# Two decode attention blocks on one core: first loads ahead of the block, x on SP's queue, the store's wait behind the closing barrier

## The chip, the cores and the metric

The kernel runs on one core of one Trainium2 chip. The core has five engines that take their instructions independently of each other: TensorE (PE), VectorE (DVE), ScalarE (ACT), GpSimd (POOL) and SyncE (SP). Here SP does nothing but issue DMAs and wait. Data are moved by 16 DMA engines. The metric is the device time of one execution in microseconds; lower is better. A profiled execution shows the span from the program's first instruction to its last; the device time holds that and what lies around it.

## What is computed

Two attention blocks, A and B, each for one new token against a cache of 8192 positions and 32 heads of 128, in bf16. Their outputs, 512 numbers each, stand side by side in the result.

```python
B, Sq, D = x.shape                     # 1, 1, 512
H, Dh = 32, 128
q = (x @ wq).reshape(B, Sq, H, Dh).transpose(0, 2, 1, 3)
scores = jnp.einsum("bhqd,bhkd->bhqk", q, k_cache) * (Dh ** -0.5)
p = softmax(scores, axis=-1)
o = jnp.einsum("bhqk,bhkd->bhqd", p, v_cache)
return o.transpose(0, 2, 1, 3).reshape(B, Sq, H * Dh) @ wo
# result: concatenate([block(A), block(B)], axis=-1)
```

B is written for grouped heads, but has as many key heads as query heads, so both blocks have one shape. Each reads 64 MB of k, 64 MB of v (in units of 2^20 bytes), 4 MB of wq and 4 MB of wo: 285 million bytes in all.

## The kernel before

**Tiling.** The 64 heads are worked through in 16 groups of four heads (n = 0 to 15, eight for A, then eight for B). A group's k, and its v, is 8 MB: four heads by 32 partitions, and 256 positions by 128 numbers on each partition. k has two buffers (`kn`, taken in turn), v has one (`vn`). The weights have no room of their own: wq of A and of B lie in `vn` until the first v comes, wo lies in a buffer of `kn` at the end, and the two rows of x (`xrow`, 1 KB each) lie on partition 0 of buffer 1 of `kn`, where the k of group 1 goes later.

**Work of a group.** DVE multiplies k by q in four chunks, in place (`plan_mul`, line 337). PE adds the products up over eight slices with an identity matrix (`plan_red`, line 346), DVE finishes the sum (line 357). Then come the maximum, the exponential on ACT (line 394), and on PE the product with v (`plan_pv`, line 415). The product with v of group n - 1 runs within the work of group n.

**The first work.** x comes in two loads that ACT issues. PE spreads each row over all partitions with a row of ones (line 297), ACT copies the result to `xb` (line 301); the second copy is the mark `x_ready`. `plan_q` multiplies `xb` by wq (line 315), 16 matmuls for four groups, and ACT copies q to `qbc` (line 323). For A this is done ahead of the first group, for B within it.

**Order of the work.** Everything is written out by hand. A small planner (`_Plan`) holds a list of instructions and waits for each engine; `op` adds an instruction, `wait` a wait on a semaphore. `dma` adds a load or a store to an engine's list, at line 244 in the profile. At the end of the kernel each list is emitted within one `Block`, to which every engine branches at its start and at whose end all five meet at a barrier (line 174 in the profile). The program has a barrier of its own ahead of the kernel's first line (line 626).

**SP's list.** wq of A, k of group 0, wq of B; then k of group 1, which waits for `x_ready`, since x lies where it goes; then in turn v of group n, which waits until the buffer is read (v of group 0 waits until q of B is made), and k of group n + 2, which waits for the reduction of group n; then wo of both blocks in pieces, the last v in two pieces, and the store. The store of the 1024 results waits for the last copy on DVE (line 488), and SP waits for the store.

```python
def load_k(n):
    k_in[n] = dma("SP", flat(kn[:, n % NK]), quad(ks, n), s_k[n % NK],
                  [x_ready if n == KX else red_done.get((n - NK, NCH - 1))])

def load_wq(a):
    wq_in[a] = dma("SP", wq_buf[a], wqs[a].rearrange("(p c) n -> p (c n)", p=P), s_w[a])
```

Of the kernel before, what the change touches and what calls it, by code (L numbers as in the profile page):

```python
# [23 lines left out]
class _Plan:  # L24
# [6 lines left out]
    def wait(self, eng, mark):  # L31
        if mark is None:
            return
        ctr, val = mark
        if val <= 0 or self.waited.get((eng, ctr.name), 0) >= val:
            return
        self.waited[(eng, ctr.name)] = val
        self.prog[eng].append((None, ctr, val))

    def op(self, eng, fn, ctr=None, needs=(), inc=1):  # L40

        for m in needs:
            self.wait(eng, m)
        self.prog[eng].append((fn, ctr, inc))
        if ctr is None:
            return None
        ctr.n += inc
        return ctr, ctr.n


def _emit(e, items, slot=None):
    for fn, ctr, k in items:
        if fn is None:
            e.wait_ge(ctr.sem, k)
        elif isinstance(fn, tuple):
            which, fns = fn
            if slot is None:
                fns[which](e).then_inc(ctr.sem, k)
            else:
                with e.If_eq(slot, 0):  # L60
                    fns[0](e).then_inc(ctr.sem, k)
                with e.Else():
                    fns[1](e).then_inc(ctr.sem, k)
        elif ctr is None:
            fn(e)
        else:
            fn(e).then_inc(ctr.sem, k)


def _steps(items):  # L70


    out, waits = [], []
    for it in items:
        if it[0] is None:
            waits.append(it[1:])
        else:
            out.append((waits, it))
            waits = []
    assert not waits  # L80
    return out
# [48 lines left out]
def bass_concat_heads__mha_block_cached__gqa_block_cached__decode_kernel(  # L130
# [13 lines left out]
    xs = [A_x, B_x]  # L144
# [4 lines left out]
    NA = 2  # L149
# [13 lines left out]
    NK = 2  # L163
# [8 lines left out]
    VLAST = (0, T - CT, T)  # L172

    with ExitStack() as st:
        ec = st.enter_context
        block = ec(nc.Block())

        def sb(name, shape, dt):
            return ec(nc.sbuf_tensor(name, shape, dt))
# [4 lines left out]
        def flat(ap):  # L184
            return ap.rearrange("p t d -> p (t d)")
# [8 lines left out]
        xrow = flat(kn[0:1, KX])[:, 0:NA * D].rearrange("p (a d) -> p a d", a=NA)  # L194
# [19 lines left out]
        NQ = NOUT // P  # L214
        yT = sb("yT", [P, NA, NQ], BF16)
        out_q = sb("out_q", [NA * NQ, P], BF16)
# [11 lines left out]
        pl = _Plan()  # L228
        op, wait = pl.op, pl.wait

        def ctr(name):
            return _Ctr(nc, st, name)

        s_x = ctr("s_x")
# [3 lines left out]
        s_v = [ctr("s_v%d" % i) for i in range(len(VLAST) - 1)]  # L238
        s_out = ctr("s_out")
# [3 lines left out]
        def dma(eng, dst, src, c, needs=()):  # L243
            return op(eng, lambda e: e.dma_start(dst, src), c, needs, inc=16)  # L244


        def const(fn, needs=()):
# [5 lines left out]
            out=ident[:], in_=ones_bf[:], pattern=[[1, P]], compare_op=ALU.is_equal,  # L253
            fill=0.0, base=0, channel_multiplier=-1), [i_onesb])
        i_identf = const(lambda e: e.affine_select(
            out=ident_f[:], in_=ones_f[:], pattern=[[1, P]], compare_op=ALU.is_equal,
# [5 lines left out]
        i_pool = const(lambda e: e.memset(pt[:], 0.0))  # L262


        x_in = [dma("ACT", xrow[0:1, a, :], xs[a][0], s_x) for a in range(NA)][-1]
        k_in, v_in, wq_in, wo_in = {}, {}, {}, {}
        red_done, pv_done, q_done, wo_done = {}, {}, {}, {}

# [4 lines left out]
# [3 lines that stand above are left out]
# [7 lines left out]
        def load_wq(a):  # L283
            wq_in[a] = dma("SP", wq_buf[a], wqs[a].rearrange("(p c) n -> p (c n)", p=P), s_w[a])

        def load_wo(a, g):
# [2 lines left out]
            wo_in[a, g] = dma("SP", wo_sb[a][:, h0:h0 + n, :].rearrange("p j n -> p (j n)"), src,  # L289
                              s_wo[a][g], [red_done[NM - 2, NCH - 1]])  # L290


        for a in range(NA):
            def xmm(e, a=a):
# [5 lines left out]
            m = op("PE", xmm, c_pe, [x_in, i_onesb])  # L300
# [29 lines left out]
        turn = [None]  # L330
# [101 lines left out]
        def plan_sel():  # L432
            for g in RG:
                v = ident[:].rearrange("p (s j) -> p s j", j=g)
                op("DVE", lambda e, g=g, v=v: e.tensor_reduce(mask[g][:], v, AX.X, ALU.max),
                   c_dve, [i_ident])
                sel_ready[g] = op("DVE", lambda e, g=g, v=v: e.tensor_reduce(
                    jsel[g][:], v.rearrange("p s j -> p j s"), AX.X, ALU.max), c_dve)
# [45 lines left out]
        def plan_out():  # L484
            m = op("PE", lambda e: e.matmul(bmp[0:NA * NQ, 0:P], yT[:].rearrange("p a q -> p (a q)"),
                                            ident[:], start=True, stop=True),
                   c_pe, [qy_free[0], nb_done[NM - 1]])
            m = op("DVE", lambda e: e.tensor_copy(out_q[:], bmp[0:NA * NQ, 0:P]), c_dve, [m])
            done = dma("SP", out[0].rearrange("o (q n) -> (o q) n", q=NA * NQ), out_q[:], s_out, [m])
            wait("SP", done)  # L490


        L0, L1 = 1, NM
        cuts = {n: [] for n in range(L0, L1 + 1)}
        dcuts = []

        load_wq(0)
        load_k(0)
        load_wq(1)
        plan_sel()  # L500
        for j in range(QA // 4):
            plan_q(0, j)
# [56 lines left out]
        for g in range(BEFORE + 1, NB):  # L559
            plan_wo(1, g)  # L560
        plan_y(1)
        plan_out()

        for name, at in (("SP", block.sync), ("PE", block.tensor), ("ACT", block.scalar),
                         ("DVE", block.vector), ("POOL", block.gpsimd)):
            @at
            def _(e, name=name):
                prog = pl.prog[name]
                if name == "DVE":
                    ends = dcuts[::NK]  # L570
                    _emit(e, prog[:ends[0]])
                    lp = _Loop(e, [prog[x:y] for x, y in zip(ends, ends[1:])])
                    with e.Fori(0, len(ends) - 1) as turn[0]:
                        for k in range(len(lp.body)):
                            lp.emit(k, None)
                    turn[0] = None
                    _emit(e, prog[ends[-1]:])
                    return
                if name != "PE":
                    _emit(e, prog)  # L580
                    return
                _emit(e, prog[:cuts[L0][0]])
                lp = _Loop(e, [prog[cuts[n][0]:cuts[n + 1][0]] for n in range(L0, L1)])
                a, b = [len(_steps(prog[cuts[L0][0]:x])) for x in cuts[L0][1:]]
                final = _steps(prog[cuts[L1][1]:cuts[L1][2]])
                assert len(final) == b - a == len(VLAST)
                for k, (ws, it) in zip(range(a, b), final):
                    assert it[1:] == lp.body[k][1][1:]
                    have = lp.last[k] + ([(s_v[k - a - 1], 16)] if k > a + 1 else [])
                    assert all(w in have for w in ws)  # L590
                slot, left = e.alloc_register("slot"), e.alloc_register("left")
                e.reg_mov(slot, L0 % NK)
                e.reg_mov(left, L1 - L0)
                with e.Fori(0, 2) as again:
                    with e.Fori(0, (L1 - L0) - (L1 - L0 - 1) * again):
                        with e.If_ne(left, 0):
                            for k in range(a):
                                lp.emit(k, slot)
                        for k in range(a, b):
                            if k > a + 1:  # L600
                                with e.If_eq(left, 0):
                                    e.wait_ge(s_v[k - a - 1].sem, 16)
                            lp.emit(k, slot)
                        with e.If_ne(left, 0):
                            for k in range(b, len(lp.body)):
                                lp.emit(k, slot)
                            e.reg_sub(slot, 1, slot)
                        e.reg_sub(left, left, 1)
                    with e.If_eq(left, -1):
                        _emit(e, prog[cuts[L1][2]:])  # L610
                    with e.Else():
                        _emit(e, prog[cuts[L1][0]:cuts[L1][1]])


# [26 lines left out]
```

## Time and profile before

| | us |
|---|---|
| median of 3 runs | 667.87 (667.80 to 667.88) |
| span of the profiled execution | 666.3 |
| PE, DVE, ACT busy in it | 440.7, 340.2, 62.4 |
| first issue of a load on SP | 0.80 |
| issue of the store | 664.67 |

The profiled execution shows 666.3 us from the first to the last instruction. Its own device time is not recorded apart from the span; the median of the runs shown lies 1.57 us above that span, and what lies in between is not in the trace. The DMA engines are busy at nine tenths or more in 39 of the 40 slices of the span.

Rows of the timeline and of the chain begin with the start in us from the span's start and the duration in us; "SPq" is an instruction of SP's sequencer, and an issue of a DMA has the time that the issuing takes, not the transfer. "To landing" is the time from the issue until the last byte is reported. A row of waits has the us in total, how often, and the longest.

### The profile page before, as it was taken

The numbers are of one execution on the slowest core, as the hardware profiler recorded it, in microseconds if no ns is written. First come the engines' busy times: TensorE is split into PE (matmuls) and PEld (weight loads), VectorE is DVE, ScalarE is ACT, GpSimd is POOL, SyncE is SP. The second block draws the span as 40 slices with busy tenths as digits, with TensorE's granted clock in tenths as the row PEclk, the third lists the DMA queues.
The fourth block names the chain that finished last, engine by engine and source line by source line (L and its number), as shares of the span: only waits on it lengthen the run. The fifth ranks groups of instructions, "written<-read, shape, count | busy, mean of one in ns | idle before, by whom it ended". The sixth has DMA issues, their size and how long they took to land.

```text
span 666.3 us, 12449 instructions
## 1 busy us (share of the span) xinstructions
PE 440.7 (66%) x5646; PEld 252.4 (38%) x5646; DVE 340.2 (51%) x215; ACT 62.4 (9%) x151; POOL 2.8 (0%) x15
## 2 busy tenths in 40 slices
PE   2065875938487594848658484865948486685866
PEld 1022352615244261614425161442626144252645
DVE  1095818356381835638083563809256481925610
ACT  1002002020201002020200202020020202002020
POOL 1000000000000000000000000000000000000000
PEclk9678777769787775978777587877658797765875
DMA  9999999999999999999999999999999999999996
GB/s 378 437 445 438 438 431 433 409 437 441 441 429 433 441 441 425 417 437 441 441 421 441 441 433 429 417 441 441 441 421 441 437 433 429 421 441 441 407 454 274
DMA packets 6076, 285.33 MB, mean 428 GB/s; under 512 B 690, under 2 KB 948, under 8 KB 1204
## 3 DMA queue, kind: packets, MB, share of 16 engines
q1 hardware_dynamic: 6064, 285.22, 99.2%
q8 instruction: 6, 0.10, 0.1%
q14 instruction: 2, 0.02, 0.0%
q10 hardware_dynamic: 4, 0.00, 0.0%
HBM read 285.21 MB, written 0.00 MB: 428 GB/s over the span
## 4 chain that ended last, share of the span: by engine, by line
DMA 62%; PE 25%; DVE 10%; issue 2%; SPq 0%; DVEq 0%; another core or an unknown queue 0%; ACT 0%
DMA kn<-in_B_k_cache_dram 21%; DMA kn<-in_A_k_cache_dram 19%; PE rps L346 15%; DMA vn<-in_A_v_cache_dram 14%; PE acc L415 10%; DVE kn L337 9%; DMA vn<-in_B_v_cache_dram 5%; DMA kn<-in_B_wo_dram 4%; SPq L244 0%; DVE s_sb L357 0%; PE qyp L315 0%; DVEq L117 0%; PE misc L399 0%; ACT qbc L323 0%
## 5 line engine op out<-in xcount | busy, mean ns | idle before, releaser
L346 PE MATMUL rps<-kn,ident 128*128 128x512 bf16 x1024 | 294.5, 456 | 171.7 <-DVE kn L337 171.7
L337 DVE TENSOR_TENSOR kn<-kn,qbc 128x8192 bf16<-128x8192 bf16 x64 | 281.5, 4419 | 98.5 <-DMA kn<-in_A_k_cache_dram 59.0
L346 PEld LDWEIGHTS rps<-kn,ident 128*128 128x128 bf16 x1024 | 112.5, 114 | 340.6 <-issue 266.3
L415 PE MATMUL acc<-pt,vn 128*128 128x4 bf16 x4096 | 108.8, 165 | 5.6 <-DMA vn<-in_B_v_cache_dram 2.4
L415 PEld LDWEIGHTS acc<-pt,vn 128*128 128x128 bf16 x4096 | 108.3, 100 | 6.2 <-DMA vn<-in_B_v_cache_dram 2.7
L357 DVE TENSOR_REDUCE s_sb<-rps 128x64 f32<-128x512 f32 x64 | 44.0, 688 | 110.9 <-PE rps L346 110.9
L394 ACT ACTIVATE pt<-s_sb,negb 32x256 bf16<-32x256 f32 x64 | 54.8, 857 | 2.1 <-ACT negb L386 0.2
L386 ACT ACTIVATE negb<-bmp 128x1 f32<-128x1 f32 x16 | 2.7, 171 | 528.8 <-PE bmp L382 528.8
L424 DVE TENSOR_TENSOR oD<-acc,rinv 128x4 f32 (+1 forms) x16 | 2.6, 163 | 90.9 <-PE acc L415 90.9
L382 PE MATMUL bmp<-gm,hrow 1*128 1x1 f32 x128 | 17.0, 249 | 6.0 <-DVE gm L372 6.0
L382 PEld LDWEIGHTS bmp<-gm,hrow 1*128 1x128 f32 x128 | 15.6, 188 | 10.7 <-DVE gm L372 10.0
L369 PE MATMUL mtp<-ident_f,m 128*1 128x128 f32 x32 | 6.1, 271 | 19.8 <-DVE m L363 19.8
L394 ACT ACTIVATION_READ_ACCUMULATOR pt<-s_sb,negb 32x1 f32 x64 | 15.9, 248 | 0.0
L369 PEld LDWEIGHTS mtp<-ident_f,m 128*1 128x1 f32 x32 | 1.4, 81 | 27.7 <-DVE m L363 27.7
L473 PE MATMUL qyp<-o,kn 128*128 128x1 bf16 x248 | 7.4, 165 | 4.9 <-issue 3.5
L315 PE MATMUL qyp<-vn,xb 128*32 128x512 bf16 x64 | 5.9, 496 | 5.8 <-DMA vn<-in_A_wq_dram 4.3
L473 PEld LDWEIGHTS qyp<-o,kn 128*128 128x128 bf16 x248 | 7.0, 102 | 5.4 <-issue 3.9
L372 DVE TENSOR_REDUCE gm<-mtp 1x4 f32<-1x128 f32 x16 | 4.5, 279 | 7.6 <-PE mtp L369 7.6
L399 PEld LDWEIGHTS misc<-rsum,ones_f 128*128 128x128 f32 x32 | 6.2, 197 | 3.5 <-issue 1.4
L363 DVE TENSOR_REDUCE m<-s_sb 128x1 f32<-128x256 f32 x16 | 6.7, 420 | 0.5
L323 ACT CAST qbc<-qyp 128x512 bf16<-128x512 f32 x4 | 2.3, 586 | 43.0 <-PE qyp L315 43.0
L297 PE MATMUL misc<-ones_bf,kn 1*128 1x128 bf16 x4 | 0.6, 302 | 8.0 <-DMA kn<-in_B_x_dram 8.0
(36 smaller groups left out, 25.1 us busy)
## 6 DMA issues: line engine op xcount, KB each, us to landing
vn<-in_B_v_cache_dram SPq DMA_DIRECT2D x1, 6144.0 KB, 22.2
vn<-in_A_wq_dram SPq DMA_DIRECT2D x1, 4096.0 KB, 12.4
vn<-in_B_wq_dram SPq DMA_DIRECT2D x1, 4096.0 KB, 40.6
kn<-in_A_wo_dram SPq DMA_DIRECT2D x1, 4096.0 KB, 35.1
kn<-in_B_wo_dram SPq DMA_DIRECT2D x1, 2048.0 KB, 39.6
vn<-in_B_v_cache_dram SPq DMA_DIRECT2D x1, 2048.0 KB, 26.7
kn<-in_B_wo_dram SPq DMA_DIRECT2D x1, 1024.0 KB, 28.7
kn<-in_B_wo_dram SPq DMA_DIRECT2D x1, 512.0 KB, 29.5
```

The costliest lines, as they stand in the source:

```text
L315: r = e.matmul(qyp[hh * HP:(hh + 1) * HP, :].rearrange("p (i d) -> p i d", d=Dh), xb[:, a, c, hh * HP:(hh + 1) * HP], w, start=(c == 0), s ...
L337: mul_done[n, c] = op("DVE", lambda e: e.tensor_tensor(k, k, qbc[:, nth(n), :].broadcast_to([P, CT, Dh]), ALU.mult), c_mul, [k_in[n], qbc_ ...
L346: r = e.matmul(rps[:, c % 2, :].rearrange("p (t d) -> p t d", d=DW), ident[:], kn[:, i0, c * CT:(c + 1) * CT, i * DW:(i + 1) * DW], start= ...
L357: sr_done[n, c] = op("DVE", lambda e: e.tensor_reduce(s_sb[:, c * CT:(c + 1) * CT], rps[:, c % 2, :].rearrange("p (t d) -> p t d", d=DW), ...
L363: m_done[n] = op("DVE", lambda e: e.tensor_reduce(m1[:], s_sb[:], AX.X, ALU.max), c_dve, [sr_done[n, NCH - 1]])
L369: m = op("PE", lambda e: e.matmul(mtp[0:1, 0:P], m1[:], ident_f[:], start=True, stop=True), c_pe, [m_done[n], i_identf, gm_done.get(n - 1)])
L372: gm_done[n] = op("DVE", lambda e: e.tensor_reduce(gm[:], mtp[0:1, 0:P].rearrange("o (h p) -> o h p", h=G), AX.X, ALU.max), c_dve, [m, nb_ ...
L382: r = e.matmul(bmp[:, 0:1], hrow[0:1, h, :], gm[0:1, h:h + 1], start=(h == 0), stop=(h == G - 1))
L394: p_done[n] = op("ACT", lambda e, h=h, q=q: e.activation(pt[q, :, h], s_sb[q, :], AF.Exp, bias=negb[q, n:n + 1], scale=scale, accum_out=rs ...
L399: m = op("PE", lambda e: e.matmul(misc[:, 0:G], ones_f[:], rsum[:], start=True, stop=True), c_pe, [p_done[n], misc_free[0]])
L415: r = e.matmul(acc[:, 0:G], vn[:, t, :], pt[:, t, :], start=(t == 0), stop=(t == T - 1))
L473: r = e.matmul(qyp[:, i:i + 1], wo_sb[a][:, j, i * P:(i + 1) * P], (o2 if n > 1 else oD)[:, a, j:j + 1], start=(j == 0 and i == 0), stop=( ...
```

## The change

The block is opened later. The list of SP is cut: what stands in it when wq of A, the two rows of x, k of group 0 and wq of B are planned is emitted ahead of the block, and the rest within it. The lists of the other engines are emitted within the block as before. The rows of x move from ACT's list to SP's, behind wq of A. The wait for the store moves from SP's list to the line behind the block, so SP goes to the closing barrier when it has issued the store. The body of the block is indented by one step more; its lines are the same otherwise, and the lines of the kernel shift by one to four.

```diff
     with ExitStack() as st:
         ec = st.enter_context
-        block = ec(nc.Block())
...
-        x_in = [dma("ACT", xrow[0:1, a, :], xs[a][0], s_x) for a in range(NA)][-1]
         k_in, v_in, wq_in, wo_in = {}, {}, {}, {}
...
+        load_wq(0)
+        x_in = [dma("SP", xrow[0:1, a, :], xs[a][0], s_x) for a in range(NA)][-1]
 
         for a in range(NA):
             def xmm(e, a=a):
...
-            done = dma("SP", out[0].rearrange("o (q n) -> (o q) n", q=NA * NQ), out_q[:], s_out, [m])
-            wait("SP", done)
+            dma("SP", out[0].rearrange("o (q n) -> (o q) n", q=NA * NQ), out_q[:], s_out, [m])
...
-        load_wq(0)
         load_k(0)
         load_wq(1)
+        ahead = len(pl.prog["SP"])
         plan_sel()
...
-        for name, at in (("SP", block.sync), ("PE", block.tensor), ("ACT", block.scalar),
-                         ("DVE", block.vector), ("POOL", block.gpsimd)):
-            @at
-            def _(e, name=name):
-                prog = pl.prog[name]
+        _emit(nc.sync, pl.prog["SP"][:ahead])
+
+        with nc.Block() as block:
+            for name, at in (("SP", block.sync), ("PE", block.tensor), ("ACT", block.scalar),
+                             ("DVE", block.vector), ("POOL", block.gpsimd)):
+                @at
+                def _(e, name=name):
+                    prog = pl.prog[name][ahead if name == "SP" else 0:]
...
+        nc.sync.wait_ge(s_out.sem, s_out.n)
```

More of the change, by code (lines that the diff above doesn't have):

```diff
@@ L562, in bass_concat_heads__mha_block_cached__gqa_block_cached__decode_kernel @@
         plan_out()
-        for name, at in (("SP", block.sync), ("PE", block.tensor), ("ACT", block.scalar),
-                         ("DVE", block.vector), ("POOL", block.gpsimd)):
-            @at
-            def _(e, name=name):
-                prog = pl.prog[name]
[L569 to L597, printed above, removed]
-                                lp.emit(k, slot)
[L599 to L612, printed above, removed]
@@ new lines, in bass_concat_heads__mha_block_cached__gqa_block_cached__decode_kernel @@
+        _emit(nc.sync, pl.prog["SP"][:ahead])
[5 more added lines that the diff above has]
+                    prog = pl.prog[name][ahead if name == "SP" else 0:]
+                    if name == "DVE":
+                        ends = dcuts[::NK]
+                        _emit(e, prog[:ends[0]])
+                        lp = _Loop(e, [prog[x:y] for x, y in zip(ends, ends[1:])])
+                        with e.Fori(0, len(ends) - 1) as turn[0]:
+                            for k in range(len(lp.body)):
+                                lp.emit(k, None)
+                        turn[0] = None
+                        _emit(e, prog[ends[-1]:])
+                        return
+                    if name != "PE":
+                        _emit(e, prog)
+                        return
+                    _emit(e, prog[:cuts[L0][0]])
+                    lp = _Loop(e, [prog[cuts[n][0]:cuts[n + 1][0]] for n in range(L0, L1)])
+                    a, b = [len(_steps(prog[cuts[L0][0]:x])) for x in cuts[L0][1:]]
+                    final = _steps(prog[cuts[L1][1]:cuts[L1][2]])
+                    assert len(final) == b - a == len(VLAST)
+                    for k, (ws, it) in zip(range(a, b), final):
+                        assert it[1:] == lp.body[k][1][1:]
+                        have = lp.last[k] + ([(s_v[k - a - 1], 16)] if k > a + 1 else [])
+                        assert all(w in have for w in ws)
+                    slot, left = e.alloc_register("slot"), e.alloc_register("left")
+                    e.reg_mov(slot, L0 % NK)
+                    e.reg_mov(left, L1 - L0)
+                    with e.Fori(0, 2) as again:
+                        with e.Fori(0, (L1 - L0) - (L1 - L0 - 1) * again):
+                            with e.If_ne(left, 0):
+                                for k in range(a):
+                                    lp.emit(k, slot)
+                            for k in range(a, b):
+                                if k > a + 1:
+                                    with e.If_eq(left, 0):
+                                        e.wait_ge(s_v[k - a - 1].sem, 16)
+                                lp.emit(k, slot)
+                            with e.If_ne(left, 0):
+                                for k in range(b, len(lp.body)):
+                                    lp.emit(k, slot)
+                                e.reg_sub(slot, 1, slot)
+                            e.reg_sub(left, left, 1)
+                        with e.If_eq(left, -1):
+                            _emit(e, prog[cuts[L1][2]:])
+                        with e.Else():
+                            _emit(e, prog[cuts[L1][0]:cuts[L1][1]])
```

## The prediction

> **What bounds the kernel now.** I read the page from its chain of waits to the DMA rows, then the stretches by stage, and last the first 50 us and the last 3 us as timelines, since the change touches nothing in between.
>
> ```profile
> span 666.3 us, 12449 instructions
> DMA  9999999999999999999999999999999999999996
> q1 hardware_dynamic: 6064, 285.22, 99.2%
> q8 instruction: 6, 0.10, 0.1%
> q10 hardware_dynamic: 4, 0.00, 0.0%
> DMA 62%; PE 25%; DVE 10%; issue 2%; SPq 0%; DVEq 0%; another core or an unknown queue 0%; ACT 0%
> vn<-in_A_wq_dram SPq DMA_DIRECT2D x1, 4096.0 KB, 12.4
> vn<-in_B_wq_dram SPq DMA_DIRECT2D x1, 4096.0 KB, 40.6
> kn<-in_B_wo_dram SPq DMA_DIRECT2D x1, 1024.0 KB, 28.7
> ```
>
> ```profile
> core 0: us, PE busy (x) PEld busy (x) DVE busy (x) ACT busy (x) POOL busy (x), PEclk, DMA share, GB/s
> 0.00:2.00 2.00, 0.00 (x0) 0.00 (x0) 0.51 (x3) 0.41 (x1) 1.38 (x9) 1.00 0.64 164
> 62.50:604.50 542.00, 373.06 (x4648) 211.75 (x4648) 293.55 (x168) 51.93 (x131) 0.00 (x0) 0.76 1.00 433
> 653.58:666.30 12.72, 9.65 (x322) 9.08 (x322) 1.06 (x5) 0.00 (x0) 0.00 (x0) 0.50 0.63 258
> ```
>
> The kernel is a stream: 285 MB pass through one queue, SP's (q1), whose packets fill 99.2% of 16 engines' span. In the 542 us between the landing of the second k group and that of the last one the DMA share is 1.00 at 433 GB/s, while PE is busy for 373 us of 542 and DVE for 294. So nothing that PE, DVE or ACT wait for in between is worth time as long as the queue holds work. The time is made of three parts: what passes before the first packet, the stream, and what passes after the last landing. The change can gain in the first and the third alone, and lose only by leaving a hole in the stream or lengthening an end.
>
> **The first loads and the start.** SP's part of the chain of waits, and the timeline of the start:
>
> ```profile
> 0.74 0.07 issue
> 0.80 0.40 SPq L244
> 631.70 0.04 issue
> 634.11 29.37 DMA kn<-in_B_wo_dram
> ```
>
> ```profile
> start us, us, engine line op out<-in xcount [idle before <-releaser]
> 0.80 0.52 ACTq L244 DMA_DIRECT2D kn<-in_A_x_dram  x1
> 0.80 0.40 SPq L244 DMA_DIRECT2D vn<-in_A_wq_dram  x1
> 1.26 0.41 SPq L244 DMA_DIRECT2D kn<-in_A_k_cache_dram  x1
> 1.35 0.21 ACTq L244 DMA_DIRECT2D kn<-in_B_x_dram  x1
> 1.73 0.42 SPq L244 DMA_DIRECT2D vn<-in_B_wq_dram  x1
> 8.01 0.61 PE L297 MATMUL misc<-ones_bf,kn 1*128 1x128 bf16 x4 [8.01 <-DMA kn<-in_B_x_dram]
> 9.14 0.59 ACT L301 CAST xb<-qyp 128x512 bf16<-128x512 f32 x1
> 9.75 0.33 SPq L244 DMA_DIRECT2D kn<-in_A_k_cache_dram  x1
> 13.36 1.93 PE L315 MATMUL qyp<-vn,xb 128*32 128x512 bf16 x16 [4.31 <-DMA vn<-in_A_wq_dram]
> 17.90 0.58 ACT L323 CAST qbc<-qyp 128x512 bf16<-128x512 f32 x1 [1.96 <-PE qyp L315]
> 32.60 8.76 DVE L337 TENSOR_TENSOR kn<-kn,qbc 128x8192 bf16<-128x8192 bf16 x2 [28.82 <-DMA kn<-in_A_k_cache_dram]
> ...
> 632.22 2.33 SPq L244 DMA_DIRECT2D kn<-in_B_wo_dram  x5
> ```
>
> SP comes out of the start-up barrier of the program (line 626) and sets off wq of A at 0.80. Only the 0.07 us of "issue" ahead of it holds the branch into the block; the barrier, which comes ahead of the block in both kernels, stays. Between two instructions that SP issues back to back stand 0.04 us (the row at 631.70). So the branch that wq no longer waits for is worth 0.07 - 0.04 = **0.03 us**. Its bounds are 0, if what stands there is the barrier's own release, and 0.07.
>
> **x behind wq.** Now x goes out on ACT's queue (q10, 4 packets) at 0.80 and 1.35, beside wq, and the later one lands at about 8.0. On SP's queue it stands behind wq, which lands at 0.80 + 12.4 = 13.2. I put x at 13.3, 5.3 us later. From x to the end of the second cast is now 8.01 to 9.14 + 0.59 = 9.73, so 1.7 us: x_ready moves from 9.73 to 15.0. Two things wait for it.
> - q of A: today its matmuls start with wq at 13.36, and the last cast of the pair ends at 17.90 + 0.58 = 18.48, 5.1 us later. From 15.0 it ends at 20.1. The first multiply (line 337) needs k, which lands at 32.60. The cover is 12.5 us and the delay 1.6, so the cost is nothing; beyond the cover every microsecond would count in full, since k of group 2 may only go where the first group has been read.
> - k of group 1, whose wait on x_ready is the same in both kernels: SP issues it at 9.75 now and at 15.1 then. In the queue it stands behind k of group 0 and wq of B, whose data end at 1.73 + 40.6 = 42.3. The engines reach it 27 us after its new issue, so no hole opens. On SP nothing is queued behind that wait but v of group 0, which needs q of B and so wq of B anyway.
>
> PE's first matmuls (line 297) wait 5.3 us longer, and what stands behind them on PE needs wq, or k, which come no earlier. ACT loses two issues and waits for the same matmuls.
>
> **What else SP issues.** The two x instructions took 0.52 and 0.21 us on ACT; with two gaps of 0.04 they hold up k of group 0 and wq of B by 0.8 us, to about 2.0 and 2.5. The engines are busy with wq until 13.2, eleven microseconds beyond that, which covers it. In the queue itself two short transfers are new. What a transfer costs there beyond its bytes can be bounded at the end of the stream: the 1024 KB piece of wo, first of the five issues whose last one starts at 634.11, is issued at 632.22 and lands 28.7 us later, at 660.92; the last piece lands at 634.11 + 29.37 = 663.48. Between them 1024 KB land, in four transfers and 2.56 us; at 433 GB/s the bytes alone take 2.42. That is 0.035 us a transfer, so 0.07 for the pair, less what the same two packets take off the engines today from the other queue. I take **0**, with 0 and +0.15 (the pair at twice that) as bounds.
>
> **The end.** The closing rows: SP's waits, the instructions of the block's exit (line 174), and the timeline.
>
> ```profile
> SPq L174 <- DMA out_dram<-out_q: 0.9, 1, 0.9
> SPq L174 <- PEq L174: 0.2, 1, 0.2
> ```
>
> ```profile
> L174 SPq COMPARE_BRANCH  x1: 33/33/33, 665.9 to 665.9; - x1
> L174 SPq DRAIN  x1: 7/7/7, 666.1 to 666.1; - x1
> L174 SPq EVENT_SEMAPHORE  x1: 17/17/17, 666.2 to 666.2; - x1
> L174 PEldq EVENT_SEMAPHORE  x1: 51/51/51, 666.2 to 666.2; - x1
> ```
>
> ```profile
> 664.36 0.28 DVE L488 CAST out_q<-bmp 8x128 bf16<-8x128 f32 x1 [0.36 <-PE bmp L485]
> 664.67 0.37 SPq L244 DMA_DIRECT2D out_dram<-out_q  x1
> ```
>
> SP issues the store from 664.67 to 665.04 and waits 0.9 us, until 665.9. Only then do its branch out of the block, its drain and the barrier of five engines follow: from 665.9 to the span's end at 666.3, **0.37 us** with the row's rounding. In the new order these 0.37 us begin at 665.04 and are over by 665.45, under the flight of the store, which lands at 665.9 as before. What remains behind the landing is one wait instruction, 0.017 to 0.051 us by the rows of the same kind. The gain is 0.37 - 0.04 = **0.33 us**. Bounds: 0, if the program's end is set by something that follows SP's last instruction at a fixed distance from the barrier, and 0.9 + 0.37 = 1.27, if it is set by what follows on the other four engines, which are free at 665.45.
>
> **The sum.** 0.03 + 0 + 0.33 = 0.36 us less: the span goes from 666.3 to 665.9. The median of the runs, 667.87, is 1.57 us above the profiled span; no view of this trace shows what lies there, so I leave it as it is, and the time becomes 667.87 - 0.36 = **667.5 us**, 0.05% less. What a measurement of this kernel can tell from no change is about 0.2%, 1.34 us: the forecast is "the same".
>
> The Trainium skill (Runtime: NRT & Kernel Launch, section "The ~15µs preamble/postamble breakdown") has a barrier behind each kernel at which all engines are waited for. By that rule the four engines that are free early gain nothing by it, as SP still comes last, and the sum stays at 667.5; without it the sum could be as low as 667.87 - 1.27 - 0.03. No run here shows that barrier.
>
> **Rivals.**
> 1. *What follows on the other engines sets the end.* PE, ACT, DVE and POOL leave the closing barrier 0.9 us earlier than the span's gain alone would have it. If their own work behind the kernel is the longest, up to 1.27 + 0.03 us go: 666.6 us. For it speaks that 1.57 us lie outside the span; against it, that SP still has to come to its end after 665.9. That is 1.30 us, just inside 0.2%.
> 2. *Nothing is saved.* The start is set by the barrier and the end by the store's landing and a fixed tail behind it: 667.9 us. For it: the store takes as long as before (0.37 + 0.9), and it is the last thing in both orders. Against it: the exit at line 174 visibly starts behind the landing now.
> 3. *Slower: an instruction fetch falls on the DMA engine that ends last.* The place: the 16 engines are 99.2% busy with the one queue, so the one with the most foreign work ends last and releases the last piece of wo at 663.48. The 6 fetches of q8 take 0.1% of 16 engines' span, 0.001 x 666.3 x 16 = 10.7 us, so 1.8 us each (0.9 to 2.7 with the rounding of 0.1%). The change moves code between ACT's and SP's programs and places instructions ahead of the block. If that leads one fetch more to that engine, the end moves by 1.8 us, less the 0.36: 669.3. It decides from the point at which the fetched engine is behind all others; on any other engine it is covered. Against it: PE's and DVE's programs, the long ones, keep their instructions and order.
> 4. *Slower: x comes too late.* If x on SP's queue took not 13.3 but more than 13.3 + 12.5 = 25.8 us, the first multiply would wait. With x 2 us beyond that point: 667.5 + 2 = 669.5. Only a queue that ends x behind k of group 0 could do that; the queue's loads land in the order of their issue (wq of A at 13.2, k at 32.6, wq of B at 42.3).
>
> The Trainium skill (Runtime: NRT & Kernel Launch, section "Instruction fetch mechanics") has instructions streamed in 16 KiB blocks by each engine's own DMA queue, and a taken branch beyond the loaded pages pay for a fetch. That is the rule behind rival 3 which speaks against moving code; q8's 0.10 MB in 6 packets agree with its block size, and the branch into the block, 0.07 us, shows no such stall.
>
> **How the numbers follow.** Forecast 0.66, own range 667.2 to 667.75 (0.07 and 0.6 us gained to the bound of the short transfers). Rival 1 0.12, rival 2 0.12, rival 3 0.08, rival 4 0.02. The range for 8 of 10 takes in the forecast, rival 2 with the bound of +0.15 and a fetch that costs only part, and most of rival 1: 666.7 to 668.2. Faster by over 0.2% (under 666.53) needs rival 1 at its full price and a stream that ends a little earlier as well: 0.06, out of rival 1's chance. Slower by over 0.2% (over 669.21) needs rival 3 at its middle price or rival 4: 0.07. The same: 0.87.
>
> **What would show it.** Right: the first issue of wq at 0.77; x landing at 13 to 14, x_ready near 15 and the first multiply still near 32.6; the second k group still landing near 62.5; the last piece of wo near 663.5; the closing barrier at 665.0 to 665.5 and the span's end within 0.1 of the store's landing. Wrong: a multiply of group 0 that waits for q instead of k; a DMA share under 1.00 between 62.5 and 604.5; a last landing of wo more than 0.3 us away from 663.48, which would be rival 3; a span shorter by 0.4 with a time that is shorter by 1 (rival 1) or not at all (rival 2).

## The result and the profile after

The changed kernel takes 666.89 us (median of 21 runs, 666.69 to 667.17), the kernel before 667.85 in the same series (21 runs, 667.63 to 668.13). The ratio is 0.9986 with a 95% interval of 0.998 to 0.9992: 0.96 us less, a gain that is clear of zero and under the 0.2% that the text ahead called "the same". 667.5 was forecast, so the direction and the class hold, but the gain is two to three times the 0.36 us of the sum. The time lies in the wide range (666.7 to 668.2) and below the forecast's own (667.2 to 667.75), towards the 666.6 of its rival 1.

The page of the changed kernel, and its stretches (the same columns as before):

```profile
span 665.6 us, 12449 instructions
q1 hardware_dynamic: 6068, 285.22, 99.2%
q8 instruction: 6, 0.10, 0.1%
```

```profile
0.00:2.00 2.00, 0.00 (x0) 0.00 (x0) 0.51 (x3) 1.21 (x1) 1.38 (x9) 1.00 0.51 131
62.50:604.50 542.00, 372.71 (x4648) 212.92 (x4648) 293.45 (x168) 51.76 (x129) 0.00 (x0) 0.75 1.00 433
```

The 4 packets of x have gone from q10 to q1, and q10 is no longer there. The stream is what it was: 1.00 at 433 GB/s over the same 542 us. The start, as a timeline:

```profile
0.80 0.38 SPq L243 DMA_DIRECT2D vn<-in_A_wq_dram  x1
1.23 0.32 SPq L243 DMA_DIRECT2D kn<-in_A_x_dram  x1
1.61 0.23 SPq L243 DMA_DIRECT2D kn<-in_B_x_dram  x1
1.89 0.36 SPq L243 DMA_DIRECT2D kn<-in_A_k_cache_dram  x1
2.29 0.53 SPq L243 DMA_DIRECT2D vn<-in_B_wq_dram  x1
13.37 0.61 PE L298 MATMUL misc<-ones_bf,kn 1*128 1x128 bf16 x4 [13.37 <-DMA kn<-in_B_x_dram]
15.12 0.33 SPq L243 DMA_DIRECT2D kn<-in_A_k_cache_dram  x1
17.17 0.59 ACT L324 CAST qbc<-qyp 128x512 bf16<-128x512 f32 x1 [2.08 <-PE qyp L316]
19.83 0.58 ACT L324 CAST qbc<-qyp 128x512 bf16<-128x512 f32 x1 [2.08 <-PE qyp L316]
32.42 8.76 DVE L338 TENSOR_TENSOR kn<-kn,qbc 128x8192 bf16<-128x8192 bf16 x2 [28.64 <-DMA kn<-in_A_k_cache_dram]
```

wq goes out at 0.80, as before: the branch that it no longer waits for was worth nothing. x lands at 13.3, k of group 1 is issued at 15.12, q of A is done at 19.83 + 0.58 = 20.41, and the first multiply still starts with k, at 32.42.

The end: the last piece of wo in the chain of waits, SP's waits, the instructions of the block's exit (now line 566), and the store in the timeline.

```profile
633.76 29.45 DMA kn<-in_B_wo_dram
```

```profile
SPq L616 <- DMA out_dram<-out_q: 0.5, 1, 0.5
SPq L566 <- PEq L566: 0.2, 1, 0.2
```

```profile
L566 POOLq EVENT_SEMAPHORE  x2: 17/17/17, 665.0 to 665.1; - x2
...
L566 SPq DRAIN  x1: 207/207/207, 664.8 to 664.8; - x1
L566 SPq EVENT_SEMAPHORE  x1: 17/17/17, 665.1 to 665.1; - x1
```

```profile
664.39 0.31 SPq L243 DMA_DIRECT2D out_dram<-out_q  x1
```

From the issue of the store to the span's end it was 666.28 - 664.67 = 1.61 us; it is 665.65 - 664.39 = 1.26. That is 0.35 less, where 0.33 was forecast. The exit of the block now lies ahead of the store's landing: POOL, whose two semaphore instructions come ahead of those of the other engines, leaves the barrier at 665.1, 0.70 us behind the issue of the store. In the kernel before it left at 666.2, 1.53 behind it:

```profile
L174 POOLq EVENT_SEMAPHORE  x2: 17/17/17, 666.1 to 666.2; - x2
```

The last piece of wo lands at 663.21, 0.28 ahead of the execution profiled before.

What the spans do not show is the rest. Each run has its time and its span. In the runs of before that went with the experiments, the span's median is 666.0 (665.8 to 666.3 in the 33 runs of the first four) and the time 1.75 us above it; in the 21 runs of the changed kernel the span's median is 665.6 and the time 1.29 above it. So 0.4 us are gone within the span, and 0.46 behind its end.

### The profile page after: what moved, and what is told of

The parts are those of the page before. It is cut to its first block, busy times and chain, and to the rows that moved or that the text cites. A ratio compares the mean times of both kernels' runs of the same rounds, so it can differ in the third digit from the quotient of the medians.

```text
span 665.6 us, 12449 instructions
## 1 busy us (share of the span) xinstructions
PE 438.8 (66%) x5646; PEld 253.2 (38%) x5646; DVE 340.1 (51%) x215; ACT 62.4 (9%) x151; POOL 2.8 (0%) x15
## 3 DMA queue, kind: packets, MB, share of 16 engines
q1 hardware_dynamic: 6068, 285.22, 99.2%
## 4 chain that ended last, share of the span: by engine, by line
DMA 66%; PE 23%; DVE 8%; issue 2%; SPq 1%; ACT 0%; DVEq 0%
DMA kn<-in_B_k_cache_dram 20%; DMA kn<-in_A_k_cache_dram 18%; DMA vn<-in_A_v_cache_dram 14%; PE rps L347 13%; PE acc L416 10%; DMA vn<-in_B_v_cache_dram 9%; DVE kn L338 8%; DMA kn<-in_B_wo_dram 4%; SPq L243 1%; PE qyp L316 0%; DVE s_sb L358 0%; ACT qbc L324 0%; PE misc L400 0%; DVEq L338 0%; PE bmp L486 0%
## 5 line engine op out<-in xcount | busy, mean ns | idle before, releaser
L347 PE MATMUL rps<-kn,ident 128*128 128x512 bf16 x1024 | 290.2, 451 | 168.0 <-DVE kn L338 168.0
```

The source lines that it names most:

```text
L347: r = e.matmul(rps[:, c % 2, :].rearrange("p (t d) -> p t d", d=DW), ident[:], kn[:, i0, c * CT:(c + 1) * CT, i * DW:(i + 1) * DW], start= ...
```

## The experiments

### Which half of the change it is

The first four kernels separate the end from the front. The first has only the wait moved:

```diff
-            done = dma("SP", out[0].rearrange("o (q n) -> (o q) n", q=NA * NQ), out_q[:], s_out, [m])
-            wait("SP", done)
+            dma("SP", out[0].rearrange("o (q n) -> (o q) n", q=NA * NQ), out_q[:], s_out, [m])
...
+        nc.sync.wait_ge(s_out.sem, s_out.n)
```

> Only the wait for the store moves behind the closing barrier; the first loads and x stay as before. Theory E (the exit gives most of it, partly behind the span): the span loses 0.36 us behind the issue of the store (1.61 before, 1.25 after the change), the rest of the time beyond the span loses 0.28 (1.57 to 1.29), so the time is 0.64 below before, near 667.2, and the gap from time to span is 1.29. Rival S (only the span's own 0.36 belongs to the exit; the 0.28 beyond it come from x leaving ACT's queue): 0.36 below, near 667.5, gap 1.57. Rival F (the gain comes from the front): within 0.1 of before.

The second is the changed kernel with the lines marked "-" put back and the wait behind the block taken out:

> The first loads ahead of the block and x on SP's queue; SP waits for the store within the block as before. Theory E: the issue of wq stays at 0.80 and nothing else is gained at the start, so what is left is the stream's end, which moves by up to 0.3 us either way with the DMA engine that ends last: 0 to 0.3 below before, 667.55 to 667.85, with the gap from time to span at 1.57. Rival S: the gap falls to 1.29 and the time to 667.6 or less. Rival F: 0.9 below, near 666.9.

The third has, of the front, only x on SP's queue, with all loads within the block:

> x on SP's queue behind wq of A, all loads within the block, SP waits within the block. Theory E: the same as the front as a whole, within 0.1 us of it, since loads ahead of the block start no earlier (0.80 in both). If the loads ahead of the block do shorten something that the profile of the start does not show, this kernel is slower than the front as a whole by that much. Last piece of wo lands within 0.3 of 663.4.

The fourth is the changed kernel in which the other four engines wait for the store as well:

```diff
-        nc.sync.wait_ge(s_out.sem, s_out.n)
+        for e in (nc.sync, nc.tensor, nc.scalar, nc.vector, nc.gpsimd):
+            e.wait_ge(s_out.sem, s_out.n)
```

> The changed kernel with a wait for the store behind the closing barrier on all five engines, not on SP alone. Theory E, with the part beyond the span due to the other four engines' being free early: the span stays at that of the changed kernel within 0.1, the gap from time to span goes from 1.29 back to 1.57, and the time is 0.28 above the changed kernel, near 667.2. If the 0.28 come from SP having no branch, drain and barrier behind its last wait, the time stays at 666.9 within 0.1.

Medians in us, with the span's median and the median of time less span, 11 runs each and 33 of before on the same chip:

| kernel | time | ratio, 95% interval | span | time less span |
|---|---|---|---|---|
| before | 667.78 | | 666.0 | 1.75 |
| wait moved only | 666.91 | 0.9987 (0.9978 to 0.9996) | 665.6 | 1.31 |
| front only | 667.66 | 0.9999 (0.999 to 1.0008) | 665.9 | 1.76 |
| x on SP's queue only | 667.73 | 1.0 (0.9991 to 1.0009) | 666.0 | 1.73 |
| all five wait | 667.43 | 0.9995 (0.9986 to 1.0004) | 665.6 | 1.77 |

The moved wait alone is the whole gain; its time is that of the changed kernel. The front is worth nothing that these runs can tell. So rivals F and S are out, S also because time less span stays at 1.73 with x on SP's queue. What comes back when all five wait, 667.43 - 666.91 = 0.52, is the part behind the span: the span keeps the gain, and time less span is again what it was before. So the time does not end a fixed way behind the last instruction. It depends on which engines that instruction holds back. The intervals of these two ratios overlap, but their runs do not: 667.36 to 667.61 with all five waiting and 666.76 to 667.08 with the wait moved only, and 1.73 to 1.85 against 1.22 to 1.35 in time less span.

Theory E was right in kind and too small in size. It counted from the 1.57 us of the text ahead, where the runs of before have 1.75. So the moved wait was expected at 667.2 and measured at 666.91, and the five waits were expected at 1.57 and 667.2 and measured at 1.77 and 667.43.

The waits of the kernel with the wait moved alone show where the 0.4 us of the span went (the columns: us in total, times, the longest):

```profile
SPq L612 <- DMA out_dram<-out_q: 0.5, 1, 0.5
SPq L562 <- PEq L562: 0.2, 1, 0.2
```

SP waits 0.5 us for the store and not 0.9, since the other 0.4 pass in the barrier; in the kernel with the front alone it is 0.9 again.

```profile
SPq L567 <- DMA out_dram<-out_q: 0.9, 1, 0.9
```

### Which engine sets the end

In four more kernels the wait behind the barrier stands on one other engine in SP's place, for instance on PE:

```diff
-        nc.sync.wait_ge(s_out.sem, s_out.n)
+        nc.tensor.wait_ge(s_out.sem, s_out.n)
```

> The changed kernel with the wait for the store behind the closing barrier on PE alone; SP ends at the barrier. Theory L (one engine has the longest way from its last instruction to the end, 1.75 us, and the others a shorter one): unless PE is that engine the time stays at the changed kernel's 666.9 within 0.1; if it is, 667.35 to 667.45, as with all five waiting. Theory A (PE, ACT, DVE and POOL all need 1.75 us, SP alone less): 667.4 for each of the four. Theory O (the engines' ends follow each other in a chain, so that the place in it counts): between 666.9 and 667.4, different for each engine.

> The same with ACT as the one that waits for the store. Theory L: 666.9 within 0.1, or 667.35 to 667.45 if ACT is the engine with the longest way. Theory A: 667.4. Theory O: in between.

> The same with DVE as the one that waits for the store. Theory L: 666.9 within 0.1, or 667.35 to 667.45 if DVE is the engine with the longest way. Theory A: 667.4. Theory O: in between.

> The same with POOL as the one that waits for the store. Theory L: 666.9 within 0.1, or 667.35 to 667.45 if POOL is the engine with the longest way. Theory A: 667.4. Theory O: in between.

| engine that waits | time (11 runs) | range | span | time less span |
|---|---|---|---|---|
| SP (the changed kernel, 21 runs) | 666.89 | 666.69 to 667.17 | 665.6 | 1.29 |
| DVE | 666.94 | 666.73 to 667.29 | 665.6 | 1.36 |
| ACT | 667.09 | 666.86 to 667.49 | 665.7 | 1.45 |
| PE | 667.24 | 667.04 to 667.34 | 665.7 | 1.55 |
| POOL | 667.42 | 667.32 to 667.60 | 665.6 | 1.81 |
| before (33 runs) | 667.76 | 667.53 to 668.00 | 666.0 | 1.74 |

Neither "one engine has the long way" (theory L) nor "all four alike" (theory A) holds. What came is what theory O had, a time between 666.9 and 667.4 that differs by engine: from the last instruction to the end of the time it takes from 1.29 us when that is SP's to 1.81 when it is POOL's. The differences in time less span between neighbours in the table are 0.07 to 0.26. Run by run POOL (1.76 to 1.85) and PE (1.52 to 1.60) stand apart from all others; ACT (1.39 to 1.49), DVE (1.33 to 1.45) and SP (1.24 to 1.36) overlap with their neighbours, and SP's runs are of another series.

With the ways in hand, the ends can be reckoned. In the kernel before, the engines leave the barrier at 666.2, 1.53 us behind the issue of the store (the row of POOL above), and the end comes 1.53 + 1.81 = 3.34 us behind that issue. In the changed kernel POOL needs 0.70 + 1.81 = 2.51, and SP 1.26 + 1.29 = 2.55: the two come out even, and the gain is 3.34 - 2.55 = 0.79 us, against 0.87 measured for the moved wait alone.

Is SP's own way 1.29, or does it look so because POOL ends at the same moment? Two kernels ask. The first has no block at all, and so neither branches nor the barrier:

```diff
-        with nc.Block() as block:
-            for name, at in (("SP", block.sync), ("PE", block.tensor), ("ACT", block.scalar),
-                             ("DVE", block.vector), ("POOL", block.gpsimd)):
-                @at
-                def _(e, name=name):
+        def rest(e, name):
...
+        for name, e in (("PE", nc.tensor), ("ACT", nc.scalar), ("DVE", nc.vector),
+                        ("POOL", nc.gpsimd), ("SP", nc.sync)):
+            rest(e, name)
```

> The changed kernel without a block at all: each engine's list is emitted behind its start, so there is no branch in and out and no closing barrier. POOL ends near 3.5 us, ACT near 645, PE and DVE near 664.3, SP with the landing of the store near 665.6. Theory P (each engine needs a time of its own from its last instruction to the end, POOL the longest, and in the changed kernel POOL's 1.77 us from the barrier set the end as much as SP's 1.29 from its wait): with POOL early, SP's own way decides, and the time falls below 666.9 by whatever that way is shorter than 1.29: 666.4 to 666.9. Theory H (the ends are handed on from POOL by way of PE, ACT and DVE to SP, 0.1 us each, with SP last): SP needs 1.29 whatever the others do, so 666.9 within 0.1. Rival G (the code without a block streams its instructions differently): the last piece of wo lands more than 0.5 us away from 663.2.

The second makes SP late, with a second store of the same numbers:

```diff
         nc.sync.wait_ge(s_out.sem, s_out.n)
+        nc.sync.dma_start(out[0].rearrange("o (q n) -> (o q) n", q=NA * NQ), out_q[:]).then_inc(s_out.sem, 16)
+        nc.sync.wait_ge(s_out.sem, s_out.n + 16)
```

> The changed kernel with a second store of the same result behind the wait, and a wait for that too, so that SP ends some 1.3 us after the landing of the first store, by the span. Both theories: the gap from time to span is then SP's own way from its last instruction to the end with the other four long done. Theory H: 1.29. Theory P: less than 1.29, by as much as the kernel without a block falls below 666.9.

Without a block: 666.91 us (11 runs, 666.71 to 667.27), span 665.7, time less span 1.24. With the second store: 668.22 (667.91 to 668.29), span 666.9, time less span 1.28. Both came out as theory H had them, and theory P's fall below 666.9 did not come. That does not show the handing on of theory H, since a way of SP's own that is as long gives the same. The last piece of wo lands at 663.14 without a block, so rival G is out too. With the second store the waits of SP show both stores:

```profile
SPq L618 <- DMA out_dram<-out_q: 0.9, 1, 0.9
...
SPq L617 <- DMA out_dram<-out_q: 0.5, 1, 0.5
```

SP's way is 1.24 to 1.28 us with the others long done, so SP alone is enough to end the changed kernel where it ends, and POOL's being free still earlier brings nothing. By the reckoning above POOL alone would end it at the same moment, so a shorter flight of the store would bring something only in a kernel that frees POOL earlier as well; that was not tried. The block itself costs nothing any more. None of the kernels that were run beats the changed one.

### How much later x could come

The prediction had x_ready 5.3 us later at no cost, and said that beyond a cover of 12.5 us each microsecond would count in full. Two kernels move x further down SP's queue, behind k of group 0 and behind wq of B. The edit of the second:

```diff
         load_wq(0)
+        load_k(0)
+        load_wq(1)
         x_in = [dma("SP", xrow[0:1, a, :], xs[a][0], s_x) for a in range(NA)][-1]
...
-        load_k(0)
-        load_wq(1)
```

> The changed kernel with x one place later on SP's queue, behind k of group 0, so that it lands near 32.5 us instead of 13.3. The first cast of q, which four groups need, ends 4.45 us behind the landing of x in the changed kernel (13.32 to 17.76), so the first multiply starts near 37.0 instead of 32.4, 4.6 late. Theory C (the prediction's sentence that beyond the cover every microsecond counts in full): 666.9 + 4.6 = 671.5. Theory Q (only a hole in SP's queue counts): the issue of v of group 0 goes from 53.7 to 58.3, and the queue holds k of group 1 until 62.6, so no hole opens: 666.9 within 0.3.

> The changed kernel with x behind wq of B, so that it lands near 42.2 us. Theory C: the first multiply starts near 46.7, 14.2 late, so 666.9 + 14.2 = 681.1. Theory Q: two holes. k of group 1 is issued near 44.0, when the queue has been empty since 42.1, and its first packet follows 1.0 later: 2.9 us. v of group 0 is issued near 53.7 + 14.2 = 67.9, when the queue has been empty since 62.6 + 2.9 = 65.5: 3.4 us. Together 6.3: 673.2, and the second k group lands near 65.5.

Behind k of group 0: 668.54 us (10 runs, 667.64 to 669.38), 1.65 over the changed kernel's 666.89. Behind wq of B: 677.05 (4 runs, 676.74 to 678.19), 10.2 over it. The timeline of the first of the two:

```profile
36.43 0.58 ACT L325 CAST qbc<-qyp 128x512 bf16<-128x512 f32 x1 [2.08 <-PE qyp L317]
...
37.12 8.76 DVE L339 TENSOR_TENSOR kn<-kn,qbc 128x8192 bf16<-128x8192 bf16 x2 [33.34 <-ACT qbc L325]
...
39.09 0.58 ACT L325 CAST qbc<-qyp 128x512 bf16<-128x512 f32 x1 [2.08 <-PE qyp L317]
...
58.48 0.33 SPq L243 DMA_DIRECT2D vn<-in_A_v_cache_dram  x1
...
98.08 0.33 SPq L243 DMA_DIRECT2D vn<-in_A_v_cache_dram  x1
```

The first multiply is 4.7 us late and waits for q, as expected, and the time takes about a third of it: the sentence of the prediction was wrong. The queue's account, nothing, was wrong too. The stretches show no hole: from 62.5 to 101 us the queue moves as much (first row) as in the changed kernel (second row).

```profile
62.50:101.00 38.50, 26.32 (x324) 14.80 (x325) 20.54 (x12) 3.62 (x9) 0.00 (x0) 0.71 1.02 436
62.50:101.00 38.50, 25.69 (x324) 14.35 (x324) 20.68 (x11) 1.54 (x4) 0.00 (x0) 0.72 1.01 434
```

What has shrunk is the lead of the issues. v of group 1 is set off at 98.08, 3.8 us before k of group 2, which stands ahead of it, lands at 101.9. In the changed kernel it is set off 8.1 us before that landing (101.7):

```profile
93.59 0.33 SPq L243 DMA_DIRECT2D vn<-in_A_v_cache_dram  x1
```

The 16 DMA engines do not end a load together, and the DMA records show small pauses of single engines here. One moves no packet from about 60.7 to 62.4, and between 99.2 and 99.9 up to three at a time are without one. Eleven packets that start between 99.2 and 100.3 take 2.7 to 3.2 us, where 2.42 is usual. Averaged over the 16 engines that is about 0.5 us more than in the changed kernel up to 115 us. The landings fall behind those of the changed kernel by 0.3 us at k of group 2 and by 0.6 up to 257 us, and stay near that. This profiled execution is the fastest of the ten (667.64). Two more lie within 0.2 us of it, and seven are slower by another 0.9 to 1.7 us, which no trace shows; it stays open.

Behind wq of B the holes are plain in the stretches:

```profile
42.00:62.50 20.50, 14.32 (x72) 5.51 (x72) 13.64 (x4) 2.24 (x4) 0.00 (x0) 1.00 0.86 358
62.50:101.00 38.50, 28.60 (x338) 15.81 (x339) 26.48 (x15) 4.79 (x11) 0.00 (x0) 0.86 0.90 381
101.00:140.00 39.00, 28.81 (x377) 17.17 (x377) 21.08 (x13) 3.62 (x9) 0.00 (x0) 0.72 0.99 429
```

```profile
44.30 0.36 SPq L243 DMA_DIRECT2D kn<-in_A_k_cache_dram  x1
47.04 8.76 DVE L340 TENSOR_TENSOR kn<-kn,qbc 128x8192 bf16<-128x8192 bf16 x2 [43.26 <-ACT qbc L326]
69.24 0.35 SPq L243 DMA_DIRECT2D vn<-in_A_v_cache_dram  x1
```

k of group 1 is issued at 44.30 with the queue dry, v of group 0 at 69.24 with the queue dry again; from 101 on all is as before. By the DMA records SP's queue moves no packet for 3.46 us from 41.8 and for 4.48 us from 65.7, together 7.9 where 6.3 were expected, partly because v was issued 1.3 later than reckoned. k of group 2 then lands 10.2 us later than in the changed kernel. The 2.3 us beyond the two pauses are in the same records. The engines do not all stop and start at once, so each stands idle for 4.06 and 4.85 us on average. And the first packet of each engine behind a pause takes 3.05 and 3.16 us on average, where 2.42 is usual: 0.6 and 0.7 more. The four add up to 10.3. With the first multiply 14.6 us late (47.04 against 32.42), "in full" would have been 14.6; the time lies between theory Q's 673.2 and theory C's 681.1.

## Why the prediction was right, and where its size was off

- **The bound.** Right. The DMA share is 1.00 at 433 GB/s over the same stretch of 542 us as before, so no wait of PE, DVE or ACT in it opened a hole.
- **The start, 0.03 us.** Its lower bound, 0, was the truth: the first issue stands at 0.80 in every kernel, with the branch ahead of it or not. The 0.07 of "issue" ahead of it are there without the branch too.
- **x behind wq, nothing.** Right in its mechanism and its numbers: x at 13.3, x_ready close to 15.0, q at 20.4 (20.1 forecast), the multiply with k. The kernel with that part alone is at 667.73 against 667.78. The cover was read too short: the 12.5 us count from the second cast of the pair, and the first multiply waits for the first one alone (with x behind k of group 0 it starts at 37.12, behind 36.43 + 0.58, and ahead of the second at 39.09). In the changed kernel the first cast ends at 17.17 + 0.59 = 17.76, so the cover is 32.42 - 17.76 = 14.7 us, and the 25.8 of rival 4 would have been 28. The sentence on what lies beyond the cover was wrong, as the two late kernels show: it is the lead of SP's issues that is used up first, at a small price, and holes in the queue that are then paid.
- **The two short transfers, 0 with +0.15 as the bound.** Right: front only is not slower than before.
- **The exit, 0.33 us.** Right as far as the span goes (0.35 from the issue of the store), and mis-sized as a term of the sum: the moved wait takes 0.87 off the time. The step that failed is the sentence that left the 1.57 us outside the span as they are. It had two faults. The 1.57 were the median time less the span of another execution; run by run the difference is 1.75. And it is no constant: it shrank to 1.29, since SP's way to the end is shorter than POOL's, which ended with it before.
- **Rival 1** named that mechanism, with 0.12, and it was the truer account. The sign that the prediction gave for it, a span shorter by 0.4 with a time shorter by 1, is what came (0.4 and 0.96). That the measured time still lies in the range for 8 of 10 is due to the room left for rival 1, not to the sum. The rival's price was wrong: 1.27 us added the flight of the store to the exit, but the other engines can leave the barrier earlier only by what the barrier itself moves, 666.3 - 665.45 = 0.85 us by the prediction's own numbers, which gives 667.0. That is near what was measured.
- **The rule that was set against rival 1.** The Trainium skill's barrier that waits for all engines (Runtime: NRT & Kernel Launch, section "The ~15µs preamble/postamble breakdown") was read as "who is free early gains nothing". The runs differ by 0.5 us with the engine that comes last, so that reading does not hold. The same section of the Trainium skill has the barrier at the start of a kernel go from engine to engine, in steps of 44 ns. An end handed on in the order POOL, PE, ACT, DVE, SP would give the order of the five ways measured, with larger steps (1.81 to 1.29 over four); no trace here shows what happens there, and the runs do not tell a chain from five ways of different length.
- **Rival 3, the instruction fetch on the last DMA engine.** It did not decide: 6 packets of q8 in both kernels, each 0.97 to 1.10 us by the DMA records (the prediction's 1.8 came from a rounded share), and the last piece of wo at 663.21 against 663.49, which lies within the 0.5 us by which the spans of before differ among themselves (665.8 to 666.3). With the wait moved only, and the front as before, it lands at 663.18. The 0.28 us between the two profiled executions are therefore not put down to the change. Rival 2 fell with the span's 0.35, rival 4 with x at 13.3.

## What to carry to other kernels

The time of this kernel does not end with its last instruction: what comes behind it depends on the engine that ran it. So the wait for the store belongs on the engine with the shortest way to the end, here SP (DVE comes within 0.1 us of it), and behind the common barrier rather than ahead of it. A span that is taken from one execution is to be subtracted from that execution's own time; a constant for "what lies around it" is only as good as the order in which the engines finish. Where one full queue sets the time, as here, a short load may come later at no cost or a small one as long as the queue stays full: what counts first is how long before the queue runs dry the next issue comes, not when its consumer starts.

## What the runs showed of the hardware that was not expected

The way from the last instruction to the end of the device time differs by the engine that runs it: 1.24 to 1.31 us for SP, 1.36 for DVE, 1.45 for ACT, 1.55 for PE, 1.81 for POOL. A queue that ran dry twice cost more than its pauses: 7.9 us without a packet went with 10.2 us of time, since the 16 engines stopped and started at different moments and the first packet of each behind a pause took 2.6 to 3.5 us instead of 2.42.
